# Moving preparation work to GpSimd and re-cutting one weight load in a decode kernel that streams its KV cache

## The chip, the cores and the metric

The kernel runs on one core of one Trainium2 chip. The metric is device time in microseconds (us) of one execution. Times are medians, with the single runs beside them where a few tenths matter.

## The reference, cut to what matters

One decode step for four sequences. Attention over a KV cache of 4096 positions and 32 heads, and a gMLP block, both read the same normalised x, and their results are added to x. All arrays are bfloat16.

```python
# B=4, Sq=1, D=640, H=32, Sk=4096, Dh=128, F=1728, Fh=864
xn = _layernorm(x)
q = (xn @ wq).reshape(B, Sq, H, Dh).transpose(0, 2, 1, 3)
scores = einsum('bhqd,bhkd->bhqk', q, k_cache) * Dh ** -0.5
o = einsum('bhqk,bhkd->bhqd', softmax(scores), v_cache)
attn = o.transpose(0, 2, 1, 3).reshape(B, Sq, H * Dh) @ wo

z = gelu(xn @ w_in)
z2 = _layernorm(z[..., Fh:])
gmlp = (z[..., :Fh] * (w_sp @ z2 + b_sp)) @ w_out      # w_out: 864 x 640
return x + attn + gmlp
```

The two caches hold 268 MB of the 282 MB that one execution reads.

## The kernel before: the parts that matter here

All loads stand in one queue, that of SyncE. The weights come first. Of the 864 rows of w_out, 768 (FA = 6 rows on each of 128 partitions) come in one transfer, the other 96 in four small transfers of eight partitions each (FR = 3 rows on a partition):

```python
FA = 6
FR = (Fh - FA * P) // 32                    # 3
w_out = at_slot(2, FA * NOUT, n_in).rearrange("p (c n) -> p c n", c=FA)
nc.sync.dma_start(out=w_out, in_=B_w_out[0:nf, :].rearrange("(p c) n -> p c n", p=P))
# [...] w_rest: a tile of 32 partitions
w_rest_d = B_w_out[nf:Fh, :].rearrange("(i r c) n -> r i c n", r=4, c=FR)
for r in range(4):
    nc.sync.dma_start(out=w_rest[r:32:4], in_=w_rest_d[r])
```

Then come the K and V units: 8.39 MB each, 64 KB on every partition, one unit for each sequence in each of four groups of eight heads. SBUF has five slots of half a unit each, and a load can be issued only when the slots of an older unit have been read. VectorE turns K by 32x32 blocks, TensorE computes the scores S and, after the group's softmax, the product O with V. The softmax of a group lies between its last K unit and its first V unit:

```python
def softmax(g):
    negmax = softmax_max(g)
    for e in range(NE):
        nc.scalar.activation(out=p_bf[:, :, e, :], in_=S_ps[:, e], func=ACT.Exp, bias=negmax[:, e:e + 1], scale=scale,
                             accum_out=rowsum[:, e:e + 1])
    # [...] transpose, copies, z_fill
    nc.tensor.matmul(cs[:], lhsT=SelP2[:].rearrange("p h e b -> p (h e b)"), rhs=rowsum[:], start=True, stop=True)
    nc.vector.tensor_tensor(out=cm[:], in0=cs[:], in1=MkG[:], op=ALU.mult)
    nc.vector.tensor_reduce(out=rinv[:], in_=cm[:], axis=AX.X, op=ALU.add)
    nc.vector.reciprocal(out=rinv[:], in_=rinv[:])

def emit_V(v):
    # [...] 64 matmuls into O_ps
    nc.vector.tensor_scalar(out=R, in0=O_ps[:, 0, :], scalar1=Mk4[:, 0:1], scalar2=None, op0=ALU.mult)
    for c in range(1, 4):
        nc.vector.scalar_tensor_tensor(out=R, in0=O_ps[:, c, :], scalar=Mk4[:, c:c + 1], in1=R, op0=ALU.mult, op1=ALU.add)
```

The end is the load of wo, the last piece of it in four cuts, and the projection that follows it:

```python
load_wo(NG - 3)
load_wo(NG - 2)
load_wo(NG - 1, (0, 4, 6, 7, 8))
# [...] matmuls with these weights, two sums, output
```

## Time and profile before

| | before |
|---|---|
| runs ahead of the change | 664.88 us median of 3 (664.66 to 665.18) |
| span in the profile | 662.6 us |
| busy: DMA engines | 98.8% of the span for the one load queue |
| busy: VectorE, TensorE, ScalarE, GpSimd | 55%, 44%, 12%, 2% |
| GB/s over the span | 427 |

The prediction below shows the lines that carry the reading: DMA slices, queues, landing times, the start, and the end of the chain. Three more lines are from the page: the busy time of each engine, then the two groups that pick O. In a group, the numbers after the bar are its busy time in us and the mean of one in ns, then the idle time ahead of it.

```profile
PE 294.1 (44%) x2283; PEld 106.3 (16%) x2283; DVE 362.5 (55%) x340; ACT 79.5 (12%) x163; POOL 10.8 (2%) x35
...
L451 DVE TENSOR_SCALAR R<-O,Mk 128x128 f32<-128x128 f32 x16 | 5.6, 351 | 122.8 <-PE O L444 122.8
...
L453 DVE SCALAR_TENSOR_TENSOR R<-O,Mk,R 128x128 f32<-128x128 f32 x48 | 16.8, 351 | 1.7
```

The reader is to note the count of VectorE's instructions, 340, and that 64 of them pick O, four for each of 16 units.

### The profile page before, as it was taken

To read this page: it belongs to the slowest core of one execution; us is meant where nothing else is said; L and a number is where in the kernel's file an instruction comes from. 1 tells how busy PE (TensorE), PEld (TensorE's weight loads), DVE (VectorE), ACT (ScalarE), POOL (GpSimd) and SP (SyncE) were. 2 spreads that over 40 slices of the span, in tenths; PEclk is the share of its full clock that TensorE was granted. 3 is DMA by queue.
4 is the path that set the end of the run, shared out by engine and by line. 5 is a ranking of instruction groups with operands and counts; after the bars stand their busy time and mean duration, and the time that the engine had idled before them with its cause. 6 is when DMAs were issued, how large, how long until landed. Compare 5 with 4: busy or idle time off the path is not lost.

```text
span 662.6 us, 5430 instructions
## 1 busy us (share of the span) xinstructions
PE 294.1 (44%) x2283; PEld 106.3 (16%) x2283; DVE 362.5 (55%) x340; ACT 79.5 (12%) x163; POOL 10.8 (2%) x35
## 2 busy tenths in 40 slices
PE   0525566266072556225446055633506254623245
PEld 0201122022021122111112022111202112211012
DVE  4338999656190849609265286745618084950002
ACT  1200000541100000530200000071110000052200
POOL 3000000000000000000000000000000000000000
PEclk9858968668577587677758596755958659667767
DMA  9999999999999999999999999999999999999996
GB/s 374 459 440 432 404 434 445 443 428 436 420 427 440 435 413 448 431 431 432 431 444 427 435 416 432 448 435 428 423 436 443 432 435 407 437 436 441 424 413 262
DMA packets 6901, 282.61 MB, mean 427 GB/s; under 512 B 808, under 2 KB 1084, under 8 KB 1500
## 3 DMA queue, kind: packets, MB, share of 16 engines
q1 hardware_dynamic: 6856, 282.25, 98.8%
q8 instruction: 18, 0.29, 0.2%
q14 instruction: 7, 0.06, 0.0%
q10 hardware_dynamic: 20, 0.01, 0.0%
HBM read 282.25 MB, written 0.01 MB: 426 GB/s over the span
## 4 chain that ended last, share of the span: by engine, by line
DMA 74%; DVE 11%; issue 11%; PE 2%; ACT 1%; SPq 0%; DVEq 0%; ACTq 0%
DMA kv<-in_A_k_cache_dram 63%; DVE kT L361 11%; DMA kv<-in_A_v_cache_dram 5%; DMA kv<-in_A_wo_dram 3%; DMA kv<-in_A_wq_dram 2%; PE O L444 2%; ACT xd L426 0%; ACT Zb L407 0%; SPq L169 0%; ACT p L415 0%; PE last_a L542 0%; DVE pT L419 0%; DVE m L379 0%; PE S L372 0%; PE misc L384 0%
## 5 line engine op out<-in xcount | busy, mean ns | idle before, releaser
L361 DVE STREAM_TRANSPOSE kT<-kv 128x2048 f32<-128x2048 f32 x128 | 282.8, 2275 | 128.5 <-DMA kv<-in_A_k_cache_dram 128.5
L372 PE MATMUL S<-kT,QZ 128*32 128x512 bf16 x1024 | 190.8, 506 | 233.3 <-DVE kT L361 233.3
L372 PEld LDWEIGHTS <-QZ 128*32 128x32 bf16 x1024 | 61.0, 111 | 357.6 <-issue 337.9
L444 PE MATMUL O<-kv,Zb 128*32 128x512 bf16 x1024 | 75.2, 458 | 58.1 <-DMA kv<-in_A_v_cache_dram 37.9
L451 DVE TENSOR_SCALAR R<-O,Mk 128x128 f32<-128x128 f32 x16 | 5.6, 351 | 122.8 <-PE O L444 122.8
L407 ACT ACTIVATE Zb<-xd,MkE 32x256 bf16<-32x256 bf16 x116 | 52.9, 498 | 108.3 <-PE O L444 106.9
L444 PEld LDWEIGHTS <-Zb 128*32 128x32 bf16 x1024 | 33.0, 113 | 99.6 <-issue 58.5
L415 ACT ACTIVATE p<-S,negmax 128x512 bf16<-128x512 f32 x8 | 5.4, 682 | 311.6 <-DVE negmax L393 311.6
L461 PE MATMUL misc<-R,SelR 128*32 128x128 f32 x32 | 6.4, 281 | 26.2 <-DVE R L453 26.2
L453 DVE SCALAR_TENSOR_TENSOR R<-O,Mk,R 128x128 f32<-128x128 f32 x48 | 16.8, 351 | 1.7
L426 DVE COPY xd<-pT 32x256 bf16<-32x256 bf16 x44 | 16.0, 364 | 0.8
L426 ACT COPY xd<-pT 32x256 bf16<-32x256 bf16 x20 | 12.2, 612 | 5.6 <-DVE pT L419 5.2
L415 ACT ACT_TABLE_LOAD x1 | 1.3, 1283 | 93.1 <-DVE negmax L393 93.1
L347 POOL COPY QZ<-qT 32x32 bf16<-32x32 bf16 x16 | 5.1, 316 | 413.4 <-PE S L372 399.8
L419 DVE STREAM_TRANSPOSE pT<-p 128x1024 bf16<-128x1024 bf16 x4 | 5.0, 1245 | 7.6 <-ACT p L415 7.6
L379 DVE TENSOR_REDUCE m<-S 128x2 f32<-128x1024 f32 x4 | 4.9, 1225 | 5.6 <-PE S L372 5.6
L461 PEld LDWEIGHTS misc<-R,SelR 128*32 128x32 f32 x32 | 2.2, 107 | 34.0 <-DVE R L453 25.3
L268 PE MATMUL q<-kv,xnT 128*32 128x512 bf16 x40 | 4.5, 631 | 5.2 <-DMA kv<-in_A_wq_dram 5.2
L384 PE MATMUL misc<-dg,ones_f 128*128 128x256 f32 x8 | 3.2, 491 | 7.5 <-DVE dg L381 7.5
L464 DVE SCALAR_TENSOR_TENSOR om<-misc,rinv,MkH 32x1024 bf16<-32x1024 f32 x4 | 5.1, 1272 | 2.0 <-PE misc L461 2.0
L430 PE MATMUL misc<-rowsum,SelP 128*32 128x2 f32 x8 | 1.1, 204 | 11.3 <-ACT p L415 11.3
L276 DVE CAST kv<-q 128x512 bf16<-128x512 f32 x1 | 0.7, 692 | 9.5 <-PE q L268 9.5
(102 smaller groups left out, 73.3 us busy)
## 6 DMA issues: line engine op xcount, KB each, us to landing
kv<-in_A_k_cache_dram SPq DMA_DIRECT2D x8, 4096.0 KB
kv<-in_A_v_cache_dram SPq DMA_DIRECT2D x1, 6144.0 KB
kv<-in_A_wq_dram SPq DMA_DIRECT2D x1, 5120.0 KB
kv<-in_A_wo_dram SPq DMA_DIRECT2D x3, 1280.0 KB
kv<-in_B_w_in_dram SPq DMA_DIRECT2D x1, 2160.0 KB, 19.9
kv<-in_A_v_cache_dram SPq DMA_DIRECT2D x1, 2048.0 KB
kv<-in_B_w_out_dram SPq DMA_DIRECT2D x1, 960.0 KB
kv<-in_A_wo_dram SPq DMA_DIRECT2D x1, 640.0 KB, 21.7
```

The source lines that it names most:

```text
L347: nc.gpsimd.tensor_copy(out=QZ[r0:r0 + 32, :, :, :, 8 + 8 * hp], in_=qT[32 * g:32 * g + 32, NE * hp:NE * hp + NE].rearrange("p e a b -> p ...
L361: nc.vector.transpose(kT[:].rearrange("p (t r) -> p t r", r=32), kw)
L372: nc.tensor.matmul(S_ps[32 * q:32 * q + 32, e], lhsT=QZ[:, b, 2 * kh + w, e, w0:w0 + 32], rhs=kb[:, i, :, e, :, w], start=(b == 0 and k < ...
L407: nc.scalar.activation(out=dst, in_=src, func=ACT.Copy, scale=mk)
L415: nc.scalar.activation(out=p_bf[:, :, e, :], in_=S_ps[:, e], func=ACT.Exp, bias=negmax[:, e:e + 1], scale=scale, accum_out=rowsum[:, e:e + 1])
L419: nc.vector.transpose(pT[:].rearrange("p t h x -> p (t h x)"), p_bf[:].rearrange("p t e m -> p (t e m)"))
L426: op(out=xd[32 * hp:32 * hp + 32, :, q, :], in_=pT[32 * q:32 * q + 32, :, hp, :].rearrange("p t x -> p x t"))
L444: nc.tensor.matmul(O_ps[32 * q:32 * q + 32, :, :], lhsT=Zb[b % 2][:, w].rearrange("p h c -> p (h c)"), rhs=vv[:, w * 4 * Dh:(w + 1) * 4 * ...
L451: nc.vector.tensor_scalar(out=R, in0=O_ps[:, 0, :], scalar1=Mk4[:, 0:1], scalar2=None, op0=ALU.mult)
L453: nc.vector.scalar_tensor_tensor(out=R, in0=O_ps[:, c, :], scalar=Mk4[:, c:c + 1], in1=R, op0=ALU.mult, op1=ALU.add)
L461: nc.tensor.matmul(oh[:], lhsT=SelR[:, b].rearrange("p h b -> p (h b)"), rhs=state["R"][:, b, :], start=(b == 0), stop=(b == B - 1))
L464: nc.vector.scalar_tensor_tensor(out=om[:], in0=oh[:, None, :].to_broadcast((G, HG, Dh)), scalar=state.pop(("rinv", g))[:, 0:1], in1=MkH[: ...
```

## The change

The intent is to take work from VectorE and ScalarE at the places where they could hold up a buffer, and to shift some bytes of w_out. There are five parts:

- w_out: 640 rows in the large transfer and 224 in the four eight-partition transfers (FA = 5, FR = 7).
- The square in the layer norm and nearly all mask building move from VectorE to GpSimd.
- In the gMLP the square, the mean's square, two scalings and the product move to GpSimd.
- The table of the exponential is loaded behind the last square root, not in the first softmax; row sums lose two VectorE operations.
- O is picked by one product with a broadcast mask and one strided reduction instead of four operations, except in the last unit.

```diff
-    FA = 6
+    FA = 5
     FR = (Fh - FA * P) // 32
@@ layer norm, masks
-    nc.vector.tensor_tensor(out=sq, in0=xc, in1=xc, op=ALU.mult)
+    nc.gpsimd.tensor_tensor(out=sq, in0=xc, in1=xc, op=ALU.mult)
-    nc.vector.tensor_reduce(out=SelP[:], in_=I32[:].rearrange("p (pr c) -> p pr c", c=C2), axis=AX.X, op=ALU.add)
+    i2 = I32[:].rearrange("p (pr c) -> p c pr", c=C2)
+    nc.gpsimd.tensor_tensor(out=SelP[:], in0=i2[:, 0], in1=i2[:, 1], op=ALU.add)
 [... SelN, SelPe, SelH, Mk4, SelR, MkE, IdF, B32 and the copy of qT in the same way ...]
@@ gMLP
-    nc.vector.tensor_tensor(out=t1, in0=z2, in1=z2, op=ALU.mult)
+    nc.gpsimd.tensor_tensor(out=t1, in0=z2, in1=z2, op=ALU.mult)
 [... msq ...]
-    nc.vector.tensor_scalar(out=t1, in0=z2, scalar1=mean[:, 0:1], scalar2=rs[:, 0:1], op0=ALU.subtract, op1=ALU.mult)
-    nc.vector.tensor_scalar(out=t1, in0=t1, scalar1=sb_f[:, 0:1], scalar2=sb_f[:, 1:2], op0=ALU.mult, op1=ALU.add)
-    nc.vector.tensor_tensor(out=z_b[:, 0, :], in0=z1, in1=t1, op=ALU.mult)
+    nc.gpsimd.tensor_scalar(out=t1, in0=z2, scalar1=mean[:, 0:1], scalar2=rs[:, 0:1], op0=ALU.subtract, op1=ALU.mult)
+    nc.gpsimd.tensor_scalar(out=t1, in0=t1, scalar1=sb_f[:, 0:1], scalar2=sb_f[:, 1:2], op0=ALU.mult, op1=ALU.add)
+    nc.gpsimd.tensor_tensor(out=z_b[:, 0, :], in0=z1, in1=t1, op=ALU.mult)
@@ exponential's table
-    nc.scalar.activation(out=etab[:], in_=eps_t[:], func=ACT.Exp)
+    nc.scalar.activation(out=etab[:], in_=rs[:], func=ACT.Exp, scale=1e-3)
@@ row sums
-    nc.tensor.matmul(cs[:], lhsT=SelP2[:].rearrange("p h e b -> p (h e b)"), rhs=rowsum[:], start=True, stop=True)
-    [... product with MkG, reduction ...]
-    nc.vector.reciprocal(out=rinv[:], in_=rinv[:])
+    for e in range(NE):
+        nc.tensor.matmul(cs[:], lhsT=SelPe[:, e].rearrange("p h e b -> p (h e b)"), rhs=rowsum[:, e:e + 1],
+                         start=(e == 0), stop=(e == NE - 1))
+    nc.vector.reciprocal(out=rinv[:], in_=cs[:])
@@ picking O
+        if v < NU - 1:
+            nc.vector.tensor_tensor(out=om4[:], in0=O_ps[:], in1=Mk4[:, :, None].to_broadcast((P, 4, Dh)), op=ALU.mult)
+            nc.vector.tensor_reduce(out=R, in_=om4[:].rearrange("p c d -> p d c"), axis=AX.X, op=ALU.add)
+        else:
+            [... the four operations as before ...]
```

More of the change, by code (lines that the diff above doesn't have):

```diff
@@ L203 @@
     xnT = const.tile([P, DC, 32], BF16)
-    nc.vector.memset(xnT[:], 0.0)
+    nc.gpsimd.memset(xnT[:], 0.0)
     nc.vector.tensor_copy(out=xnT[:, :, 0:B], in_=xT_ps[:])
@@ L214 @@
     for q in range(4):
-        nc.vector.tensor_copy(out=I32[32 * q:32 * q + 32, :], in_=ident_f[32 * q:32 * q + 32, 32 * q:32 * q + 32])
+        nc.gpsimd.tensor_copy(out=I32[32 * q:32 * q + 32, :], in_=ident_f[32 * q:32 * q + 32, 32 * q:32 * q + 32])
     I4 = const.tile([P, 4, 32], F32)
@@ L220 @@
     SelP = const.tile([P, HP * B], F32)
-    nc.vector.tensor_reduce(out=SelP[:], in_=I32[:].rearrange("p (pr c) -> p pr c", c=C2), axis=AX.X, op=ALU.add)
+    i2 = I32[:].rearrange("p (pr c) -> p c pr", c=C2)
+    nc.gpsimd.tensor_tensor(out=SelP[:], in0=i2[:, 0], in1=i2[:, 1], op=ALU.add)
     SelN = const.tile([P, HP * B], F32)
-    nc.vector.tensor_scalar(out=SelN[:], in0=SelP[:], scalar1=-scale, scalar2=None, op0=ALU.mult)
-    SelP2 = const.tile([P, HP, NE, B], F32)
-    nc.vector.tensor_copy(out=SelP2[:], in_=SelP[:].rearrange("p (h b) -> p h b", b=B)[:, :, None, :].to_broadcast((P, HP, NE, B)))
+    nc.gpsimd.tensor_scalar(out=SelN[:], in0=SelP[:], scalar1=-scale, scalar2=None, op0=ALU.mult)
+    SelPe = const.tile([P, NE, HP, NE, B], F32)
+    nc.gpsimd.memset(SelPe[:].rearrange("p x h e b -> p (x h e b)"), 0.0)
+    for e in range(NE):
+        nc.gpsimd.tensor_copy(out=SelPe[:, e, :, e, :], in_=SelP[:].rearrange("p (h b) -> p h b", b=B))
     SelH = const.tile([P, HG], F32)
-    nc.vector.tensor_reduce(out=SelH[:], in_=I32[:].rearrange("p (h c) -> p h c", c=4), axis=AX.X, op=ALU.add)
+    i2 = SelP[:].rearrange("p (h c) -> p c h", c=2)
+    nc.gpsimd.tensor_tensor(out=SelH[:], in0=i2[:, 0], in1=i2[:, 1], op=ALU.add)
     Mk4 = const.tile([P, 4], F32)
-    nc.vector.tensor_reduce(out=Mk4[:], in_=I32[:].rearrange("p (h c) -> p c h", c=4), axis=AX.X, op=ALU.add)
+    h4 = const.tile([P, 24], F32)
+    nc.gpsimd.tensor_tensor(out=h4[:, 0:16], in0=I32[:, 0:16], in1=I32[:, 16:32], op=ALU.add)
+    nc.gpsimd.tensor_tensor(out=h4[:, 16:24], in0=h4[:, 0:8], in1=h4[:, 8:16], op=ALU.add)
+    nc.gpsimd.tensor_tensor(out=Mk4[:], in0=h4[:, 16:20], in1=h4[:, 20:24], op=ALU.add)
     SelR = const.tile([P, B, HG, B], F32)
@@ L233 @@
     for b in range(B):
-        nc.vector.tensor_copy(out=SelR[:, b, :, b], in_=SelH[:])
+        nc.gpsimd.tensor_copy(out=SelR[:, b, :, b], in_=SelH[:])
     MkE = const.tile([P, NE], F32)
-    nc.vector.tensor_reduce(out=MkE[:], in_=I32[:].rearrange("p (e m) -> p e m", e=NE), axis=AX.X, op=ALU.add)
-    IdF = const.tile([P, P], F32)
-    nc.vector.tensor_copy(out=IdF[:].rearrange("p (x q) -> p q x", q=4), in_=ident_f[:].rearrange("p (q x) -> p q x", q=4))
-    MkH = const.tile([G, HG], F32)
-    nc.vector.tensor_reduce(out=MkH[:], in_=ident_f[:G, :G].rearrange("p (h b) -> p h b", b=B), axis=AX.X, op=ALU.add)
-    MkG = const.tile([G, NE], F32)
-    nc.vector.tensor_reduce(out=MkG[:], in_=MkH[:].rearrange("p (h e) -> p e h", e=NE), axis=AX.X, op=ALU.add)
-    B32f = const.tile([G, B], F32)
-    nc.vector.tensor_reduce(out=B32f[:], in_=ident_f[:G, :G].rearrange("p (h b) -> p b h", b=B), axis=AX.X, op=ALU.add)
+    h2 = const.tile([P, 2 * NE], F32)
+    i2 = SelH[:].rearrange("p (e x c) -> p c e x", e=NE, c=2)
+    nc.gpsimd.tensor_tensor(out=h2[:].rearrange("p (e x) -> p e x", e=NE), in0=i2[:, 0], in1=i2[:, 1], op=ALU.add)
+    i2 = h2[:].rearrange("p (e c) -> p c e", e=NE)
+    nc.gpsimd.tensor_tensor(out=MkE[:], in0=i2[:, 0], in1=i2[:, 1], op=ALU.add)
+    IdF = const.tile([P, P], F32)
+    nc.gpsimd.tensor_copy(out=IdF[:].rearrange("p (x q) -> p q x", q=4), in_=ident_f[:].rearrange("p (q x) -> p q x", q=4))
+    MkH = SelH[:G]
     B32 = const.tile([G, B], BF16)
-    nc.vector.tensor_copy(out=B32[:], in_=B32f[:])
+    nc.gpsimd.tensor_copy(out=B32[:], in_=Mk4[:G])
     NW = T // 4
@@ L278 @@
     qT = const.tile([P, HG, 4, B], BF16)
-    nc.vector.tensor_copy(out=qT[:], in_=q4[:, 1, :].rearrange("p (h k r) -> p h k r", h=HG, k=4)[:, :, :, 0:B])
+    nc.gpsimd.tensor_copy(out=qT[:], in_=q4[:, 1, :].rearrange("p (h k r) -> p h k r", h=HG, k=4)[:, :, :, 0:B])
     w_z = w_in.rearrange("p c (a f) -> p c a f", a=2)
@@ L316 @@
     msq = const.tile([P, 1], F32)
-    nc.vector.tensor_tensor(out=msq[:], in0=mean[:], in1=mean[:], op=ALU.mult)
+    nc.gpsimd.tensor_tensor(out=msq[:], in0=mean[:], in1=mean[:], op=ALU.mult)
     var = const.tile([P, 1], F32)
@@ L428, in softmax @@
         z_fill(g, 1)
-        cs = misc_ps([G, NE], F32)
-        nc.tensor.matmul(cs[:], lhsT=SelP2[:].rearrange("p h e b -> p (h e b)"), rhs=rowsum[:], start=True, stop=True)
-        cm = small.tile([G, NE], F32, tag="cm")
-        nc.vector.tensor_tensor(out=cm[:], in0=cs[:], in1=MkG[:], op=ALU.mult)
+        cs = misc_ps([G, 1], F32)
+        for e in range(NE):
+            nc.tensor.matmul(cs[:], lhsT=SelPe[:, e].rearrange("p h e b -> p (h e b)"), rhs=rowsum[:, e:e + 1],
+                             start=(e == 0), stop=(e == NE - 1))
         rinv = small.tile([G, 1], F32, tag="rinv")
-        nc.vector.tensor_reduce(out=rinv[:], in_=cm[:], axis=AX.X, op=ALU.add)
-        nc.vector.reciprocal(out=rinv[:], in_=rinv[:])
+        nc.vector.reciprocal(out=rinv[:], in_=cs[:])
         state[("rinv", g)] = rinv
@@ L450, in emit_V @@
         R = state["R"][:, b, :]
-        nc.vector.tensor_scalar(out=R, in0=O_ps[:, 0, :], scalar1=Mk4[:, 0:1], scalar2=None, op0=ALU.mult)
-        for c in range(1, 4):
-            nc.vector.scalar_tensor_tensor(out=R, in0=O_ps[:, c, :], scalar=Mk4[:, c:c + 1], in1=R, op0=ALU.mult, op1=ALU.add)
+        if v < NU - 1:
+            om4 = ppool.tile([P, 4, Dh], F32, tag="p", name="om4")
+            nc.vector.tensor_tensor(out=om4[:], in0=O_ps[:], in1=Mk4[:, :, None].to_broadcast((P, 4, Dh)), op=ALU.mult)
+            nc.vector.tensor_reduce(out=R, in_=om4[:].rearrange("p c d -> p d c"), axis=AX.X, op=ALU.add)
+        else:
+            nc.vector.tensor_scalar(out=R, in0=O_ps[:, 0, :], scalar1=Mk4[:, 0:1], scalar2=None, op0=ALU.mult)
+            for c in range(1, 4):
+                nc.vector.scalar_tensor_tensor(out=R, in0=O_ps[:, c, :], scalar=Mk4[:, c:c + 1], in1=R,
+                                               op0=ALU.mult, op1=ALU.add)
         if b + 2 < B:
```

## The prediction

What no trace or run of this case showed is cut from the recorded text, at the marks: a paragraph of general statements, the times that the moved operations would take on GpSimd (the square of the layer norm, five operations of the gMLP), and the two counts made from them in the second rival. The sum still came to -0.38 us, all of it from w_out and worked out from packet records, with 0 for every other part: 664.88 - 0.38 = 664.5. The normalised x "within 1 us", the gMLP's end "near 35" and "some 10 us busier" for GpSimd were estimates, which no trace supported.

"Engines 0 to 7" and "lower half" are names for the eight chains that carry w_rest in the trace of before: 32 packets of 3840 bytes, four on each of eight chains and never more than eight under way at once. "Engines 8 to 15" and "upper half" are the other eight. No record gives an engine's number. The packets of 4 bytes show the same count: in that trace each transfer of 128 partitions at the start (wq, w_in, w_out) has 16 of them, and the four of w_rest have 32, eight each.

> **What bounds the kernel now.** I began with the page's slices of the span, the queue table below them and the SyncE side of the waits, because a kernel that reads 282 MB is likely to be waiting for memory.
>
> ```profile
> DMA  9999999999999999999999999999999999999996
> GB/s 374 459 440 432 404 434 445 443 428 436 420 427 440 435 413 448 431 431 432 431 444 427 435 416 432 448 435 428 423 436 443 432 435 407 437 436 441 424 413 262
> q1 hardware_dynamic: 6856, 282.25, 98.8%
> q8 instruction: 18, 0.29, 0.2%
> q14 instruction: 7, 0.06, 0.0%
> ```
>
> The reader is to see that the 16 DMA engines are busy in every slice but the last, and that one queue alone accounts for 98.8% of their time. The compute engines are far from that: 55% for VectorE, 44% for TensorE, 12% for ScalarE, 2% for GpSimd. The question for each compute part is therefore whether it can ever make that queue run dry. The view of the line that loads the caches answers it:
>
> ```profile
> DMA to landing us min/median/max: 29.2/29.8/30.2
> ```
>
> One whole cache unit is 8.39 MB. At 27.05 GB/s for each of 16 engines (in the packet records a 40,960-byte packet takes 1514 ns) it needs 8.39 MB / 433 GB/s = 19.4 us. It lands 29.2 us after its issue at the soonest, so each load waits at least 9.8 us behind loads issued before it. A buffer may come free 9.8 us later, or any amount sooner, and no byte moves at another time. That holds for the slow stage too, the softmax ahead of a group's first V product. The two ends of the kernel have no such queue, so I read them by timeline. The start, on the engines the change touches:
>
> ```profile
> 10.87 0.17 DVE L205 COPY xnT<-misc 128x20 bf16<-128x20 bf16 x1 [0.45 <-PE misc L202]
> ...
> 16.01 4.46 PE L268 MATMUL q<-kv,xnT 128*32 128x512 bf16 x40 [5.17 <-DMA kv<-in_A_wq_dram]
> ...
> 31.16 0.48 DVE L327 STREAM_TRANSPOSE kv<-kv 128x288 bf16<-128x288 bf16 x1
> ...
> 43.38 17.66 DVE L361 STREAM_TRANSPOSE kT<-kv 128x2048 f32<-128x2048 f32 x8 [11.74 <-DMA kv<-in_A_k_cache_dram]
> ```
>
> The normalised x is ready at 11.0 and the query projection waits until 16.0 for wq. The gMLP ends on VectorE at 31.6, and VectorE is then idle for 11.74 us, until the first K unit lands. So the preparation has 5.2 us of room before the projection and over 11 us before the first transpose. The end, from the chain that ended last:
>
> ```profile
> 637.10 21.14 DMA kv<-in_A_wo_dram
> 658.24 0.04 issue
> 658.28 0.43 PE last_a L542 x2
> 658.72 0.83 PE last_a L542 x4
> ```
>
> The last weights land (658.24 for the next-to-last piece, about 658.7 for the last), TensorE uses them, and some 4 us of sums and the output transfer follow, to 662.6. What sets the time is the moment at which the slowest of the 16 engines delivers its last packet of wo.
>
> **Which engine that is.** The packet records have no engine number, but each engine takes its next packet within a few ns of the end of the one before, so they can be strung into 16 chains. The chains stop between about 654.3 and 658.65 us, a spread of over 4 us with almost equal bytes. The last 0.65 us holds packets of two chains only. The spread comes from the instruction queue: its 18 blocks each hold one data engine up for about 1.5 us (a gap near 1.05 us, and the next packet some 0.5 us long). Followed from start to end they go round about eight of the engines in a fixed order, near 37, 85, 136, 163, 199, 236, 265 and 308 us, then again from 346 and a third time from 635. Eighteen over eight means that two engines get three blocks, those met near 37 and 85 us. At the start I can tell the engines apart: half of them carry the four small transfers of w_rest and begin the first K unit about 0.6 us later (first 65,536-byte packets at 22.46 to 22.96 us, against 21.97 to 22.17 and one straggler). Both chains delayed at 37 and 85 us lie in the half that does not carry w_rest. By this reading the two last engines are in the half with fewer bytes. The chains run close to each other in places and may have been swapped near 138 us, so I give the reading 7 in 10.
>
> [...]
>
> **The change part by part.**
>
> *w_out.* Before, each engine takes 8 packets of 7680 bytes (291 ns each) and engines 0 to 7 also 4 of 3840 (149 ns). From these two sizes a packet costs 7 ns plus its bytes at 27.04 GB/s, so 6400 bytes take 244 ns and 8960 take 338. Engines 0 to 7: 8 x 291 + 4 x 149 = 2.92 us before, 8 x 244 + 4 x 338 = 3.30 after, so +0.38 us. Engines 8 to 15: 2.33 before, 1.95 after, so -0.38 us. Bytes and packet counts are unchanged; 10 KB per engine move from one half to the other. If the two latest engines are in the upper half, they end 0.38 us sooner, near 658.27. The latest in the other half end near 657.66 and, 0.38 later, still end before that. Gain 0.38 us.
>
> *Layer norm and masks.* The square of 640 columns moves to GpSimd[...]. VectorE is rid of some 20 mask operations, about 2 us in the trace. Net effect on xnT at 11.0: within 1 us, in front of 5.2 us of room: 0.
>
> *gMLP.* Columns go from 288 to 384. The square, msq, two scalings and the product cost 0.45 + 0.16 + 0.43 + 0.43 + 0.46 = 1.9 us on VectorE[...]. Wider reductions and the six more projection matmuls add under 1 us. The stage ends near 35 instead of 33, ahead of 43.4: 0. qT's copy on GpSimd moves K unit 1's issue by some 0.2 us, with 20 us of K unit 0 in the queue: 0.
>
> *Exponential's table.* The first softmax loses one 1.28 us load, now paid near 31 us when ScalarE is idle. Hidden by the 9.8 us: 0.
>
> *Row sums.* Two VectorE operations of 0.11 and 0.14 us go, a few tiny matmuls come: 0.
>
> *Picking O.* Four operations of 0.351 us, 1.5 us with their gaps, become two of 512 columns. From 0.43 us at 256 columns and 1.23 at 1024 I estimate 0.70 each, 1.4 in all. Saved 0.1 us on each of 15 units, none on the path; the last unit keeps the old form.
>
> The sum is -0.38 us: 664.88 - 0.38 = 664.5.
>
> **The rivals.** First, the last engines may be in the lower half: the same sum with the other sign, 665.26. For it speaks that this half has more bytes already; against it, where the blocks of 37 and 85 us fell. Second, GpSimd may become the bound of the preparation. It would need 5 us more before the projection, or 10 in the gMLP[...]. Even a 3 us miss leaves 664.5. Third, the operations saved on VectorE and ScalarE, some 5 us in all, may come through, giving 660. Against it stand the 9.8 us of queue before every load; I give it 1%. Fourth, other instruction counts may move the blocks to other times, so that another engine is last: anything from -0.5 to +0.7 us.
>
> **Range and chances.** The three runs before lie within 0.52 us. The sign of 0.38 and the place of the fetches give another 0.7 to either side of 664.5: 664.0 to 665.3. Two per cent is 13.3 us; nothing here comes near it in either direction.
>
> **What would show it.** The packet records should have 128 packets of 6400 bytes near 244 ns and 32 of 8960 near 338. The halves at the first K packet should part by 1.35 us instead of 0.6. The chain's last wait for wo should end near 657.9, with the same 4.4 us after it. Whole loads should still land in 29 to 30 us; the table load should be gone from the first softmax, and GpSimd some 10 us busier. The prediction is wrong if the last packet comes later than 658.65, if any load lands in about 20 us (a dry queue), or if the queue's bandwidth differs in the middle of the span.

## The result, and the profile after

The two kernels were timed on one chip, six runs each. Before: 664.85 us (664.40 to 665.18). Changed: **664.23 us** (664.09 to 664.29). The ratio is 0.999, with a 95% interval of 0.9978 to 1.0003. A ratio here is the mean time of one kernel's runs over that of the other's in the same rounds, so it is not quite the ratio of the medians. The interval is some 0.8 us wide to either side, wider than the effect looked for. But all six runs of the changed kernel lie below all six of the kernel before.

One caution for the two profiles: the profiled execution of before was its fastest (664.37 us), that of the changed kernel took 664.25. The two pages thus differ by only 0.1 us. Differences of ends are therefore read below from all profiled executions, not from this pair alone.

From the page of the changed kernel: busy times, DMA by slice, the queues, and the two groups that now pick O.

```profile
PE 292.9 (44%) x2297; PEld 106.5 (16%) x2297; DVE 360.1 (54%) x275; ACT 78.4 (12%) x162; POOL 20.3 (3%) x64
...
DMA  9999999999999999999999999999999999999996
...
q1 hardware_dynamic: 6856, 282.25, 98.8%
q8 instruction: 18, 0.29, 0.2%
q14 instruction: 7, 0.06, 0.0%
...
L458 DVE TENSOR_TENSOR om<-O,Mk 128x512 f32<-128x512 f32 x15 | 10.4, 692 | 109.0 <-PE O L449 109.0
...
L459 DVE TENSOR_REDUCE R<-om 128x128 f32<-128x512 f32 x15 | 15.3, 1019 | 0.5
```

The DMA engines are still busy in every slice, with the same packets and bytes. GpSimd has 20.3 us of work instead of 10.8. VectorE has 275 instructions instead of 340 but only 2.4 us less work: a pick of O takes 692 + 1019 = 1711 ns, more than the four operations of 351 ns, 1404 ns, that it replaces.

The landing times of whole cache units in the changed kernel (the view of the line that loads them):

```profile
DMA to landing us min/median/max: 29.2/29.7/29.8
```

The start of the changed kernel, from the timeline (start, duration, engine, line, operation; in brackets the idle time ahead of it and what ended it):

```profile
9.15 0.17 DVE L205 COPY xnT<-misc 128x20 bf16<-128x20 bf16 x1 [0.52 <-PE misc L202]
...
15.96 4.46 PE L274 MATMUL q<-kv,xnT 128*32 128x512 bf16 x40 [6.92 <-DMA kv<-in_A_wq_dram]
...
31.26 1.28 ACT L338 ACT_TABLE_LOAD   x1
31.61 1.66 POOL L330 TENSOR_SCALAR kv<-kv,mean,rs 128x384 f32<-128x384 f32 x1 [0.90 <-DVE rs L329]
...
35.15 0.58 DVE L333 STREAM_TRANSPOSE kv<-kv 128x384 bf16<-128x384 bf16 x1 [3.71 <-POOL kv L332]
...
43.41 6.70 DVE L367 STREAM_TRANSPOSE kT<-kv 128x2048 f32<-128x2048 f32 x3 [7.68 <-DMA kv<-in_A_k_cache_dram]
```

The normalised x is ready at 9.3 us (before 11.0), and the projection still waits for wq until 16.0. The gMLP ends on VectorE at 35.7 instead of 31.6, and VectorE is then idle for 7.68 us instead of 11.74, until the same 43.4. The exponential's table is loaded at 31.3 beside GpSimd's work; no such load stands in the first softmax any more.

The end of the changed kernel, from its chain of waits (start, duration, what):

```profile
635.85 22.32 DMA kv<-in_A_wo_dram
658.17 0.04 issue
658.21 0.43 PE last_a L553 x2
658.65 0.82 PE last_a L553 x4
```

The chain's last wait for wo ends at 658.17, where it ended at 658.24 before (the prediction expected about 657.9). It is the landing of the next-to-last piece. The last packet of all lands at 658.57 (658.65 before).

### The profile page after: what moved, and what is told of

It reads as the page before. It is cut to its first block, busy times and chain, and to the rows that moved or that the text cites. A ratio compares the mean times of both kernels' runs of the same rounds, so it can differ in the third digit from the quotient of the medians.

```text
span 662.5 us, 5421 instructions
## 1 busy us (share of the span) xinstructions
PE 292.9 (44%) x2297; PEld 106.5 (16%) x2297; DVE 360.1 (54%) x275; ACT 78.4 (12%) x162; POOL 20.3 (3%) x64
## 3 DMA queue, kind: packets, MB, share of 16 engines
q1 hardware_dynamic: 6856, 282.25, 98.8%
## 4 chain that ended last, share of the span: by engine, by line
DMA 74%; DVE 11%; issue 11%; PE 2%; ACT 1%; SPq 0%; DVEq 0%; ACTq 0%
DMA kv<-in_A_k_cache_dram 64%; DVE kT L367 11%; DMA kv<-in_A_v_cache_dram 5%; DMA kv<-in_A_wo_dram 3%; DMA kv<-in_A_wq_dram 2%; PE O L449 2%; ACT xd L432 0%; ACT Zb L413 0%; ACT p L421 0%; DVE pT L425 0%; PE last_a L553 0%; DVE m L385 0%; PE S L378 0%; SPq L169 0%; PE misc L390 0%
## 5 line engine op out<-in xcount | busy, mean ns | idle before, releaser
L378 PE MATMUL S<-kT,QZ 128*32 128x512 bf16 x1024 | 187.9, 500 | 230.6 <-DVE kT L367 230.6
L449 PE MATMUL O<-kv,Zb 128*32 128x512 bf16 x1024 | 73.6, 451 | 58.2 <-DMA kv<-in_A_v_cache_dram 38.0
L458 DVE TENSOR_TENSOR om<-O,Mk 128x512 f32<-128x512 f32 x15 | 10.4, 692 | 109.0 <-PE O L449 109.0
L449 PEld LDWEIGHTS <-Zb 128*32 128x32 bf16 x1024 | 32.9, 112 | 97.4 <-issue 55.8
L459 DVE TENSOR_REDUCE R<-om 128x128 f32<-128x512 f32 x15 | 15.3, 1019 | 0.5
L461 DVE TENSOR_SCALAR R<-O,Mk 128x128 f32<-128x128 f32 x1 | 0.4, 351 | 12.5 <-PE O L449 12.5
L475 DVE SCALAR_TENSOR_TENSOR om<-misc,rinv,SelH 32x1024 bf16<-32x1024 f32 x4 | 5.1, 1271 | 2.0 <-PE misc L472 2.0
L437 PE MATMUL misc<-rowsum,SelPe 128*32 128x1 f32 x16 | 2.1, 202 | 9.0 <-ACT p L421 9.0
```

Of the source, the lines that this page charges most:

```text
L378: nc.tensor.matmul(S_ps[32 * q:32 * q + 32, e], lhsT=QZ[:, b, 2 * kh + w, e, w0:w0 + 32], rhs=kb[:, i, :, e, :, w], start=(b == 0 and k < ...
L449: nc.tensor.matmul(O_ps[32 * q:32 * q + 32, :, :], lhsT=Zb[b % 2][:, w].rearrange("p h c -> p (h c)"), rhs=vv[:, w * 4 * Dh:(w + 1) * 4 * ...
L458: nc.vector.tensor_tensor(out=om4[:], in0=O_ps[:], in1=Mk4[:, :, None].to_broadcast((P, 4, Dh)), op=ALU.mult)
L459: nc.vector.tensor_reduce(out=R, in_=om4[:].rearrange("p c d -> p d c"), axis=AX.X, op=ALU.add)
L475: nc.vector.scalar_tensor_tensor(out=om[:], in0=oh[:, None, :].to_broadcast((G, HG, Dh)), scalar=state.pop(("rinv", g))[:, 0:1], in1=MkH[: ...
```

## The experiments

In the ten profiled executions that did not run their load queue dry, the device time is 5.64 to 5.78 us more than the end of the last wo packet, counted from the start of the span. So that packet's end is used below beside the times. Kernels of one batch ran on one chip beside nine runs of the kernel before. Its medians were 664.60, 664.58 and 664.56 us in the three batches.

### Each half of the change alone, first batch

Only the rows of w_out move, in the kernel before:

```diff
-    FA = 6
+    FA = 5
```

> The kernel before with the one number FA changed from 6 to 5: only the loading of w_out differs. Theory A (the spread of w_out's rows over the DMA engines is all that the change is worth): 0.4 to 0.6 us below the kernel before, near 664.3. Theory B (the shorter preparation, the fewer VectorE instructions or the table load are worth the time): the same as before, within 0.2 us. Either way the packet records should have 128 packets of 6400 bytes near 244 ns and 32 of 8960 near 338.

Everything but the rows, in the changed kernel:

```diff
-    FA = 5
+    FA = 6
```

> The changed kernel with FA back at 6: everything of the change except the loading of w_out. Theory A: no gain over the kernel before, within 0.2 us of 664.85. Theory B: the whole gain, near 664.2.

Measured: the rows alone 664.70 us (664.70, 665.94, 666.38, 664.68, 664.51), ratio 1.0011; the rest alone 664.63 (664.57 to 664.75), ratio 1.0000. Before was 664.60 (664.50 to 664.96). **Neither half gains anything alone.** The last wo packet ended at 658.95 and 659.06. The end of the chain's wait for wo, with the rows alone:

```profile
637.01 21.56 DMA kv<-in_A_wo_dram
658.57 0.04 issue
```

and with the rest alone:

```profile
634.50 24.17 DMA kv<-in_A_wo_dram
658.66 0.04 issue
```

Both waits end later than the changed kernel's 658.17. The prediction had the whole gain in the rows, so its account cannot be complete.

### w_rest spread over all engines, and all of w_out by small transfers, same batch

The kernel before, with the 96 rows in one 32-partition transfer, so that the upper half gets some of these bytes:

```diff
-    w_rest_d = B_w_out[nf:Fh, :].rearrange("(i r c) n -> r i c n", r=4, c=FR)
-    for r in range(4):
-        nc.sync.dma_start(out=w_rest[r:32:4], in_=w_rest_d[r])
+    nc.sync.dma_start(out=w_rest, in_=B_w_out[nf:Fh, :].rearrange("(p c) n -> p c n", c=FR))
```

> The kernel before with the 96 rows of w_rest loaded by one transfer of 32 partitions, so that all 16 engines carry the same bytes of w_out: 2.63 us each instead of 2.92 (engines 0 to 7) and 2.33 (8 to 15). Theory A: the upper half ends 0.30 us later and still ends last, so 0.3 us above the kernel before, near 665.15. Theory B: the same as before. If the lower half were the last one in most executions, 0.3 us below, near 664.55.

Measured 665.33 us (665.08, 665.36, 665.33, 666.09, 665.31), 0.73 above before's median, last packet 659.44. The direction is right: with bytes put on the upper half the kernel is longer, as it must be if an upper-half engine bounds it. The size is not: +0.30 was expected. The first K packet of 15 of the 16 engines took 0.29 to 0.44 us longer in this run than the usual 2.42 us, in both halves, and one engine was still on w_rest at 23.8 us. Together with the 0.30 that would make up the 0.73, but why those packets were longer stays open, so the run supports the reading without proving it. The page has 792 packets under 512 bytes where that of before has 808: this fits 16 packets of 4 bytes for the one transfer of w_rest instead of 32 for the four, that is, all 16 engines. In its trace the chain of packets that ends last has 16 KB instruction blocks near 37, 347 and 635 us, as the prediction describes its last engine.

The changed kernel with w_out wholly on the lower half:

```diff
-    nc.sync.dma_start(out=w_out, in_=B_w_out[0:nf, :].rearrange("(p c) n -> p c n", p=P))
+    w_out_d = B_w_out[0:nf, :].rearrange("(i r c) n -> r i c n", r=16, c=FA)
+    for r in range(16):
+        nc.sync.dma_start(out=w_out[r:P:16], in_=w_out_d[r])
```

> The changed kernel with all 864 rows of w_out loaded by eight-row transfers: the bytes are the same, but engines 0 to 7 carry all of them (16 x 244 + 4 x 338 ns = 5.26 us each, against 3.30 in the changed kernel) and engines 8 to 15 none. Theory A: the lower half ends last by far, 1.95 us after its end in the changed kernel, less the margin between the halves there (0 to 0.6 us): 1.4 to 1.95 us above it, 665.6 to 666.2. Theory B (the end does not depend on which engine carries what): the same as the changed kernel, near 664.2.

Measured 677.19 us, ratio 1.0188. The experiment says nothing of its question, because its design was at fault. From its windows (us, then busy time and instruction count of PE, PEld, DVE, ACT and POOL, granted clock, DMA share, GB/s):

```profile
20.00:30.00 10.00, 0.44 (x7) 0.00 (x0) 1.94 (x2) 0.59 (x1) 1.55 (x5) 0.70 0.23 68
```

The queue ran dry. The small transfers waited for w_in to land, were issued one after the other from 21.1 to 30.8 us, and the first K unit was issued at 32.9 us instead of 16.6. DMA engines were busy for 23% of that stretch. That each of the 16 transfers went to eight engines fits the page: 920 packets under 512 bytes where the changed kernel has 808, eight for each of the 16 where the one transfer had 16.

### The same again on another chip, with the changed kernel beside them

> The changed kernel once more, unaltered, beside its two halves on one chip. Before, it stood at 664.23 against 664.85 (six runs each). Theory A (the rows of w_out are worth 0.4 us and nothing else is): 0.4 to 0.6 us below the kernel before. Theory C (differences below half a us come from where the instruction blocks fall among the engines, and change with any alteration of the program or with the chip): anything within 0.6 us of the kernel before.

> The loading of w_out alone, a second time; the first time it was 0.1 us above the kernel before (664.70 against 664.60). Theory A: within 0.2 us of the changed kernel. Theory C: again near the kernel before, and 0.3 us or more above the changed kernel.

> Everything but the loading of w_out, a second time; the first time it equalled the kernel before (664.63 against 664.60). Theory A: equal to the kernel before within 0.2 us. Theory B (the compute parts are worth the time): near the changed kernel.

| batch 2 | us, median | runs | last wo packet |
|---|---|---|---|
| before | 664.58 | 664.45 to 665.64 (nine) | not profiled |
| changed | **664.17** | 664.14, 664.18, 664.17, 664.14, 664.18 | 658.47 |
| rows alone | 664.61 | 664.57, 665.13, 664.61, 664.55, 664.73 | 658.82 |
| rest alone | 664.62 | 664.66, 664.35, 664.63, 664.31, 664.62 | 658.88 |

The ratios are 0.999 (0.9976 to 1.0003), 0.9998 and 0.9995. Again the halves alone gain nothing (two runs of the rest alone come close) and both together gain 0.4 us. All five runs of the changed kernel lie below all nine of before. Over both comparisons, the eleven runs of the changed kernel lie at 664.29 or below, and the 33 runs of before in all batches at 664.40 or above (its profiled execution, which is not among them, took 664.37).

In this batch I also tried to move bytes at the end of the kernel, by splitting two of the wo loads into 112 + 8 + 8 partitions:

```diff
     def load_wo(g, c_cuts=(0, HG)):
+        if len(c_cuts) == 2 and g in (1, 2):
+            for p0, p1 in ((0, 112), (112, 120), (120, 128)):
+                nc.sync.dma_start(out=wo_t[g][p0:p1], in_=wo_q[g][p0:p1])
+            return
```

> The changed kernel with two of the four loads of wo split into 112 partitions (seven rows of 10240 bytes for each of 16 engines) and two times eight rows: the bytes are the same, and with 385 ns a row engines 0 to 7 get 2 x 0.385 = 0.77 us more and engines 8 to 15 0.77 us less. This is the clean form of the run with all of w_out on eight engines, which ran its queue dry at the start. If the end is set by the engine that is loaded most (theory A): 0.77 us above the changed kernel less the margin between the halves there, so +0.4 to +0.77. If it does not matter which engine carries what: the same as the changed kernel. If the upper half still ended last in the changed kernel by a wide margin: below it.

Measured 673.88 us, ratio 1.0136, again a fault of the design. From the waits of its queue (who waits, for what: us in all, how many, longest):

```profile
SPq L173 <- DMA kv<-in_A_v_cache_dram: 17.5, 2, 8.8
```

Two issues waited 17.5 us for V loads to land. Besides, many packets of 10,240 bytes took 619 to 836 ns instead of 389. The small transfers here take eight neighbouring partitions. The kernel's own w_rest takes every fourth partition, and its packets move 8960 bytes in 338 ns. But in the run with all of w_out in small transfers the same w_rest packets took 456 ns in the median, so packets on the same partitions can take different times. What slows them was not shown; no run separates the causes. The expected spread over the engines fits the count of packets: 840 under 512 bytes where the changed kernel has 808, which is 16 for each transfer of 112 partitions and eight for each of the four small ones, 64 where the two whole loads had 32.

### A theory for both halves together

The 16 engines end at different times, so the last of two groups of engines decides. In the profile of before I strung the packets into 16 chains again, this time by the cheapest assignment over the whole span. (Such a chain is one engine's packets in order, and not the page's chain of waits.) The latest chain, at 658.65, is in the upper half; another, at 658.61, is in the *lower* half. They tie.

The lower one was held up not only by bytes but by instruction blocks of a second kind, those of q14. Every one of these blocks is 8 KB, and its record lasts 309 to 392 ns in these ten profiles. By the stringing, the ones that VectorE's instructions need all fall on the same lower-half engine, and each costs it 0.90 to 0.99 us in the trace of before (0.97 is used below): a gap of 0.31 to 0.33 us and a next packet that is 0.59 to 0.66 us longer. These blocks seem to come by instruction count. VectorE had 467 rows in the trace of before (the page's 340 and the rows that it does not count) and had blocks at 61.4, 236.4, 426.9 and 597.3 us, when 64, 192, 312 and 438 of these rows had begun. The changed kernel, with 406 rows, has only three: at 93.4, 266.9 and 507.4 us, when 66, 176 and 320 rows had begun. So the count at which a block comes is not quite the same in the two kernels. The other blocks make up the same seven, since one more came near 275 us, probably GpSimd's (71 of its 86 rows had begun; before has 56 in all), on another engine. The 18 blocks of 16 KB seem to be TensorE's: in the trace of before 257 of its rows begin between two of them in the mean (144 to 344).

| | upper half's latest | lower half's latest | later of the two | last packet measured |
|---|---|---|---|---|
| before | 658.65 (read) | 658.61 (read) | 658.65 | 658.65 (its fastest run) |
| rows alone | 658.65 - 0.38 = 658.27 | 658.61 + 0.38 = 658.99 | 658.99 | 658.95, 658.82 |
| rest alone | 658.65 | 658.61 - 0.97 = 657.64 | 658.65 | 659.06, 658.88 |
| both | 658.27 | 658.02 | 658.27 | 658.57, 658.47 |

The ends of the chains can be read without stringing the whole span, and they agree: before has two engines within 0.04 us of each other at the end, but with the rest alone the second engine ends at 657.66 and 657.79 (the two profiles), more than 1 us ahead of the last, as it must if one of the tied two had been freed of 0.97 us. With both parts the second ends at 658.26 and 658.13. The two rows in which the upper half ends last (rest alone, both) come out 0.2 to 0.4 us early, probably since they start from the fastest run of before, but their difference holds: 658.97 to 658.52 in the mean, 0.45 us, where 0.38 was worked out. If the theory is right, the smaller count of VectorE instructions is a cause in itself, whatever those instructions cost.

### The count of instructions alone, third batch

The test adds tiny copies to the changed kernel after each pick of O: five each, 80 in all, to bring the fourth block back, and one each, 16 in all, which adds instructions without reaching it.

```diff
+        pad = small.tile([P, 1], F32, tag="pad", name="pad")
+        for _ in range(5):          # the other kernel: range(1)
+            nc.vector.tensor_copy(out=pad[:], in_=R[:, 0:1])
```

> The changed kernel with five copies of one column after each picking of O: 80 tiny VectorE instructions that nothing waits for. The trace has 467 VectorE rows before and 406 after[...] the change took the fourth block away, and here, with 486, it is back. Theory D (two engines tie at the end of the kernel before: one of the upper half with three TensorE instruction blocks, one of the lower half with four VectorE blocks; the w_out rows unload the first by 0.38 us, the fewer VectorE instructions unload the second by one block of 0.97 us, and only both together end sooner): eight small blocks instead of seven, the engine with the VectorE blocks ends near 659.0, and the time is 0.4 to 0.6 us above the changed kernel, as with the w_out part alone (664.6 to 664.7). Theory C (differences below half a us have no traceable cause): no consistent rise beyond 0.2 us.

> The same with one copy instead of five: 16 more VectorE instructions, 422 rows[...]. Theory D: seven small blocks, the same as the changed kernel within 0.1 us (664.1 to 664.3). If the added instructions themselves cost time, a fifth of what the run with 80 shows.

Measured is that the fourth block of before came when 438 rows had begun; the two kernels here have 486 and 422 rows.

Measured: with 80 copies 664.65 us (664.91, 664.65, 664.66, 664.60, 664.54), ratio 1.0000; with 16 copies **664.14** (664.19, 664.04, 664.23, 664.03, 664.14), ratio 0.9993 (0.998 to 1.0005). Before was 664.56 (664.45 to 664.93). From the page of the kernel with 80 copies:

```profile
q14 instruction: 8, 0.07, 0.0%
...
L467 DVE COPY pad<-R 128x1 f32<-128x1 f32 x80 | 12.2, 152 | 2.6
```

and from its chain:

```profile
636.81 22.02 DMA kv<-in_A_wo_dram
658.83 0.04 issue
```

From the page of the kernel with 16 copies:

```profile
q14 instruction: 7, 0.06, 0.0%
```

and from its chain:

```profile
635.07 22.94 DMA kv<-in_A_wo_dram
658.01 0.04 issue
```

With 80 copies an eighth block appears, VectorE's blocks fall at 93.4, 262.0, 425.2 and 595.5 us, the last packet ends at 659.21, and the whole gain is gone. With 16 copies there are seven blocks, VectorE's at 93.1, 266.6 and 473.2, the last packet ends at 658.41, and the gain is kept. The difference of the last packets is 0.80 us; the table gives 658.02 + 0.97 = 658.99 against 658.27, 0.72. The 12.2 us of added VectorE work are the rival, and they do not explain it: none of the loads that the landing view lists lands faster than 29.3 us after its issue with 80 copies, against 28.7 with 16, and the first V load after the first softmax, which has the least room (shown further below), still had 2.1 us of it, more than in the kernel before. The queue did not run dry.

A second rival is in the traces. With 80 copies that first V load was issued 1.2 us later than with 16 (135.23 against 134.03 us), and one of its first packets took 1.06 us longer than usual, which is as much as a block costs. It is not on the engine that decides: strung into chains by gap and by size, this packet falls to an upper-half chain that ends at 656.64. The chain that ends last, at 659.21, lost nothing there; it is in the lower half, and it holds all four of VectorE's blocks. So in this pair of kernels the block, and not the late load, is what the last engine lost.

### How much work the softmax can take before the queue runs dry, same batch

The prediction said that every load has at least 9.8 us of room. This was tested by repeating the 1.2 us reduction ahead of each softmax, six and twelve times, in the changed kernel:

```diff
+        dly = small.tile([P, NE], F32, tag="dly")
+        for _ in range(6):          # the other kernel: range(12)
+            nc.vector.tensor_reduce(out=dly[:], in_=S_ps[:].rearrange("p e t m -> p e (t m)"), axis=AX.X, op=ALU.max)
```

> The changed kernel with six more reductions of the scores (1.23 us each) in VectorE's chain of every softmax, which makes that chain 5 to 7.4 us longer. Theory (each whole load waits 9.8 us or more in the queue, so the compute parts are hidden): the same as the changed kernel within 0.5 us, although VectorE does 30 us more work. Rival (the chain of waits through VectorE is part of the time): 20 to 30 us more.

> The same with twelve reductions, 11 to 14.8 us more in the chain of every softmax. Theory: now past the room of about 10 us, the queue runs dry once in each of the four groups, for up to 5 us; 2 to 18 us above the changed kernel, and some loads land sooner than 29 us after their issue. If the room is larger than the landing times say: still the same time.

Measured 666.66 us (666.41 to 666.92), ratio 1.0031, for six, and 689.75 (688.83 to 690.43), ratio 1.0378, for twelve. Six cost 2.5 us over the changed kernel's 664.17, although 29 us of VectorE work were added: the queue ran dry once, in the first group, from about 139.2 to 141 us. Twelve cost 25.6 us, and the queue ran dry in all four groups. From the windows of the kernel with twelve, in the first and the third group, with the columns as above:

```profile
140.00:150.00 10.00, 6.42 (x64) 2.37 (x64) 2.74 (x10) 6.97 (x16) 0.00 (x0) 0.54 0.30 106
460.00:475.00 15.00, 6.80 (x68) 2.62 (x70) 7.75 (x15) 11.50 (x25) 0.00 (x0) 0.61 0.56 220
```

The DMA share falls to 0.30 and 0.56 where the changed kernel has 1.00 and 0.98. So there is room, but in the first group it is not 9.8 us: at most 7.4 us of added chain already empties the queue there.

These two kernels also bear on the count of instructions. With six reductions VectorE has 430 rows and seven 8 KB blocks; with twelve it has 454 rows and an eighth block, at 684.0 us, when 448 rows had begun.

The reason can be seen at the first V load after the first softmax. The SyncE timeline of before has the issue of that load:

```profile
136.00 0.33 SPq L161 DMA_DIRECT2D kv<-in_A_v_cache_dram  x1
```

and the same line of the changed kernel:

```profile
134.40 0.33 SPq L161 DMA_DIRECT2D kv<-in_A_v_cache_dram  x1
```

The load's first packet began at 138.1 and 137.7 us, so its room was 1.8 us in before and is 3.0 us now. The load is issued 1.6 us sooner; the 1.28 us of the table load that left this softmax would be most of that. No other load of a cache unit has less than about 5 us.

## Why the prediction was right, and where it was not

The time (664.23 and 664.17 us against 664.5), the range and the class were right. The size of the gain, 0.41 us in the second comparison and 0.62 in the first, is near the 0.38 predicted. The account of it was half right, so that the size came out near is in part luck.

- **Cost of the w_out packets: right.** The changed kernel has 128 packets of 6400 bytes at 244 ns and 32 of 8960 at 338 ns. At the first K packet the halves part by about 1.2 us (means of 21.87 and 23.11 us, one straggler of the upper half left out), where 1.35 was expected and 0.6 was read before.
- **Preparation hidden: right.** It moved by -1.7 us (normalised x) and +4.1 us (gMLP) and nothing after it moved. The prediction's "near 35 instead of 33" does not fit its own line, which has 31.6 for the end before. Measured, the square of the layer norm took 1.24 us on GpSimd (0.81 on VectorE before), and in the gMLP, now 384 columns instead of 288, the square took 0.83, msq 0.19, the two scalings 1.66 and 0.67 and the product 0.99, 4.3 us in all where VectorE took 1.9. The copy of qT took 0.29 us (0.20 on VectorE). The difference between the two scalings, of one shape, stays unexplained.
- **Picking O: the size was wrong.** The estimate was 0.70 for each of two operations; the product took 0.69 and the reduction 1.02, which reads 512 columns with a stride (in the same trace a reduction of 384 contiguous columns took 0.55). The step added 0.2 us of work or so to each unit rather than saving 0.1. Being off the path, it cost nothing.
- **"The latest in the other half end near 657.66": wrong.** This is the step that failed: the margin of 1 us between the two halves was not there. One chain of the lower half ended at 658.61, tied with the upper one. My first stringing had swapped chains, a risk that the prediction named. With the true value, the rows alone put 0.38 us on an engine that already ties for the last, and two experiments found no gain from them.
- **"The sum" with 0 for all parts but w_out: wrong, though the total was near.** The rest contributed the missing half. Not by its 5 us of saved work, which was the third rival and was rightly given 1%, but by its smaller number of VectorE instructions: one block of 8 KB is not fetched, and 0.97 us leaves the lower engine. That is close to the fourth rival, which had the blocks move and not vanish, and which I had as noise and not as part of the sum. The runs show that neither half is enough, that the count alone takes the gain away, and that 16 copies, too few to bring the block back, do not. That it is the lower-half engine that ties is read from chains without engine numbers. The reading is firm for the kernel with 80 copies and weaker for the rows alone, and which engine ends last in the changed kernel is not certain.
- **"Each load waits at least 9.8 us": wrong as a rule.** The landing view lists only some loads (27 of the 37 of this line), evidently not the one right after the first softmax. And the landing is that of the slowest engine, so the 9.8 us also count the spread of the engines as room: the K load issued at 189.0 us in before began at 196.5, after 7.5 us. The load that matters had 1.8 us of room, much less than the text says. In before, several first packets of that load were 0.3 to 0.7 us longer, 3.0 us in sum over the engines, and 0.25 us in the changed kernel; by the stringing the two chains that tie at the end lost 0.33 and 0.36 us there. In the first profile of the rows alone, some engines even stood idle for about 1 us at this load. So the earlier load may be a further gain of the rest, but it is not enough by itself: the rest alone has it and was no faster. This may be why single runs of 665 to 666.4 us occur only in kernels with the old softmax (before, rows alone, w_rest spread), while the ten runs of the rest alone stay at 664.75 or below. It fits, but no run tests it.

No version was found that beats the changed kernel by a clear margin: the one with 16 more copies is at 664.14, within the runs of the changed kernel.

## What to carry to other kernels

When DMA binds a kernel, as here (98.8% of the span in its load queue), look for the latest of the 16 engines, and count the bytes and the instruction blocks of each engine. Here the engines ended between about 654.3 and 658.65 us with nearly equal bytes; each block of 16 KB held one up for about 1.5 us and each block of 8 KB for 0.6 to 1.0 us. Where two engines tie (658.65 and 658.61 us here), each remedy alone can look useless, and only both together show. A count of instructions can matter on an engine that is not the bottleneck (VectorE, 54% busy, where 80 tiny copies stood at 664.65 us and 16 at 664.14), so test it apart from busy time, with tiny copies. Take the room of a load from its own issue and its own first packet (1.8 us for one load here), not from the landing times of other loads (which gave 9.8); and when a load is split into small transfers, see first that the queue cannot run dry while they are issued (here the DMA share fell to 0.23 for 10 us, and the time rose to 677.19 us).
